# Decode attention with a gated block: the weight loads at the start cut into other pieces

## Chip, cores and metric

The kernel runs on one core of a Trainium2 chip. The core has five engines with an instruction stream each (TensorE "PE", VectorE "DVE", ScalarE "ACT", GpSimd "POOL", SyncE "SP") and sixteen DMA engines that move data between device memory (HBM) and on-chip memory. The metric is the device time of one execution in microseconds, the median of several runs.

## What is computed

One decode step for a batch of 8 tokens: a layer norm, attention of each token over the last 2048 positions of its key and value cache (32 query heads, 8 key heads), and a gated two-layer block whose result gates the attention's output. Everything large is bf16.

```
xn = layernorm(x)                                   # x: 8 x 1 x 512
q  = xn @ wq                                        # 512 x 4096, 32 heads of 128
k, v = k_cache[:, :, 6144:], v_cache[:, :, 6144:]   # 8 x 8 x 2048 x 128 each, used by 4 heads
s  = (softmax(q k^T / sqrt(128)) v) @ wo            # 4096 x 512
h  = sigmoid(xn @ w_gate) * (xn @ w_up)             # 512 x 1792
g  = silu(h @ w_down)                               # 1792 x 512
out = x + s * g
```

## The kernel before

**Loads.** All large loads are issued by SyncE (`q0`), in the order of a list `todo` written out by hand; only the small input x is issued by ScalarE (`q1`). A load of the list is issued when `pump` reaches it. Large tiles live in nine slots of 32 KB per partition (`slots`, `empty`); `free` gives a slot back when its last reader has been emitted, and `pump` then issues the next loads.

The list begins with the gated block's weights: `w_gate` (L171), `w_up` (L172), the first 11 x 128 rows of `w_down` (L173), and the remaining 384 rows of `w_down` in eight small loads (L174 to L183), between which lie the two halves of `wq` (L181). Then come the 16 tiles of the key cache and the 16 of the value cache, 2 MB each, the value tiles three places behind (L184 to L190), and at last `wo` in four pieces (L191).

`want_rows` (L96) takes a weight with `per` consecutive rows on each partition, and loads rows r0 to r1 of every partition, in steps of `step` rows. For `w_gate` and `w_up` there are four rows of 1792 per partition, and the step is 2: two loads of 2 x 1792 x 2 = 7168 bytes per partition each.

`want_side` (L122) loads one of the eight small parts of `w_down` into the tile `side`. A small part has 3, 5 or 9 partitions, each of 15 rows (15 KB) or 4 rows (4 KB); `sides` (L174) holds them as tuples. GpSimd clears the first 32 partitions of `side` before the first of them (L126), and that first small load waits for it.

**Semaphores.** Each load signals its completion on one of eight semaphores, taken in turn by all loads (x first). A load waits until the previous load on its semaphore has landed, besides the reader that frees its slot. So a load can only be issued when the one eight places ahead of it has landed.

**Compute.** The layer norm runs first (L212 to L242); then `g_ps` = gate (L278), `u_ps` = up (L294), the turning of h (L328), q (L352) and the down projection (L366). After that a loop over the batch (L647) transposes keys (L456), computes scores (L474), exponentials (L494) and the products with the values (L584). The output projection (L706) ends the kernel, when the last piece of `wo` is there.

Of the kernel before, what the change touches and what calls it, by code (L numbers as in the profile page):

```python
# [10 lines left out]
def kernel(  # L11
# [21 lines left out]
    KT = D // P  # L33
# [59 lines left out]
        empty.append(int(t[1][4:]))  # L93
        pump()

    def want_rows(name, w, per, r0, r1, step=None):  # L96
        def f(tag):
            t = slots.tile([P, r1 - r0, w.shape[1]], bf16, name=name, tag=tag)
            for a in range(r0, r1, step or r1 - r0):
                z = a + (step or r1 - r0)  # L100
                q0.dma_start(
                    out=t[:, a - r0 : z - r0, :],
                    in_=w.rearrange("(p r) n -> p r n", r=per)[:, a:z, :],
                )
            rows_of[(name, r0)] = (t, tag)
            for r in range(r0, r1):
                weights[(name, r)] = t[:, r - r0, :]

        todo.append((True, f))

    LOW, SF = (5, 5, 3, 3), 15
    MID, SM = 9, 4
    SP = 4 * max(LOW)
    M_AT = 32
    MP = 4 * MID
    MT = 11
    m0 = MT * P
    m1 = m0 + SF * sum(LOW)
    assert m1 + SM * MP == F
    side = {}  # L120

    def want_side(w, q, at, count, rows, base, of):  # L122
        def f(tag=None):
            if tag:
                t = slots.tile([P, SF, w.shape[1]], bf16, name="side", tag=tag)
                nc.gpsimd.memzero(t[:M_AT])  # L126
                side["t"] = t
                rows_of[("side", 0)] = (t, tag)
                for r in range(SF):
                    weights[("wd_sb", MT + r)] = t[: M_AT + MP if r < SM else SP, r]  # L130
            q0.dma_start(  # L131
                out=side["t"][at + q : at + q + 4 * (count - 1) + 1 : 4, :rows].rearrange(
                    "p s n -> p (s n)"
                ),
                in_=w[base : base + of * count * rows, :].rearrange(
                    "(p q s) n -> q p (s n)", q=of, s=rows
                )[q % of],
            )

        todo.append((not side, f))  # L140
        side["asked"] = True

    def want_down(w):
        def f(tag):
            t = slots.tile([P, MT, w.shape[1]], bf16, name="wd_sb", tag=tag)
            q0.dma_start(
                out=t[:].rearrange("p t n -> p (t n)"),
                in_=w[: MT * P, :].rearrange("(p t) n -> p (t n)", t=MT),
            )
            rows_of[("wd_sb", 0)] = (t, tag)  # L150
            for r in range(MT):
                weights[("wd_sb", r)] = t[:, r, :]

        todo.append((True, f))
# [13 lines left out]

    RT = 32
    Z = 32  # L170
    want_rows("wg_sb", B_w_gate, KT, 0, KT, 2)  # L171
    want_rows("wu_sb", B_w_up, KT, 0, KT, 2)  # L172
    want_down(B_w_down)  # L173
    sides = []  # L174
    for q in range(4):
        sides.append((q, 0, LOW[q], SF, m0 + q // 2 * 2 * LOW[0] * SF, 2))
        sides.append((q, M_AT, MID, SM, m1, 4))
    for x in sides[:2]:
        want_side(B_w_down, *x)
    for i in range(2):  # L180
        want_rows("wq_sb", A_wq, KT, 2 * i, 2 * i + 2)  # L181
        for x in sides[2 + 3 * i : 5 + 3 * i]:
            want_side(B_w_down, *x)  # L183
    order = [(b, i) for b in range(B) for i in range(NQ)]  # L184
    AHEAD = 3
# [5 lines left out]
    for t0, t1 in ((0, 16), (16, 26), (26, 30), (30, RT)):  # L191
# [15 lines left out]
        out=perm[:].rearrange("k (l p) -> k l p", l=G),  # L207
        in_=ident[:].rearrange("k (p l) -> k l p", l=G),
# [11 lines left out]
        out=rstd[:], in_=mv[:, 1:2], func=AF.Sqrt, bias=eps_t[:], scale=1.0  # L220
# [4 lines left out]
        out=xn_bf[:],  # L225
# [8 lines left out]
    for kt in range(KT):  # L234
        nc.tensor.transpose(  # L235
            out=xnT_ps[:, kt, :],
            in_=xn_bf[:].rearrange("b (p kt) -> b kt p", kt=KT)[:, kt, :],
# [25 lines left out]
    with nc.allow_low_precision(reason="zeros and a one"):  # L263
        nc.vector.reduce_sum(
            out=band[:], in_=ident[:].rearrange("k (q t) -> k q t", t=RT), axis=AX.X
        )
        nc.vector.reduce_sum(
            out=pick[:], in_=ident[:].rearrange("k (q t) -> k t q", t=RT), axis=AX.X
# [22 lines left out]
    for k in range(F // FC):  # L291
        u_ps = ps_t.tile([B, FC], f32, name="u_ps", tag="t")
        for kt in range(KT):
# [8 lines left out]
            out=h_bf[:B, k * FC : (k + 1) * FC],  # L302
# [6 lines left out]
    for h in range(2):  # L309
        c = LOW[2 * h]  # L310
        at = m0 + h * 2 * LOW[0] * SF
        nc.gpsimd.tensor_copy(
            out=h_side[:, :, : 4 * c].rearrange("b t (e q) -> b t e q", q=4)[
                :, :, :, 2 * h : 2 * h + 2
            ],
            in_=h_bf[:B, at : at + 2 * c * SF].rearrange(
                "b (e q t) -> b t e q", q=2, t=SF
            ),
        )
    nc.gpsimd.tensor_copy(  # L320
        out=h_side[:, :SM, M_AT:],
        in_=h_bf[:B, m1:F].rearrange("b (p t) -> b t p", t=SM),
    )
    cuts = [h_bf[:B, :m0].rearrange("b (p t) -> b t p", t=MT)[:, t] for t in range(MT)]
    rows = [P] * MT + [M_AT + MP] * SM + [SP] * (SF - SM)
    cuts += [h_side[:, t, : rows[MT + t]] for t in range(SF)]
    for t, x in enumerate(cuts):
        nc.tensor.transpose(  # L328
            out=hT_ps[: rows[t], t, :], in_=x, identity=ident[:B, :B]
# [45 lines left out]
    for e in range(2):  # L375
# [3 lines left out]
        for r in range(rep):  # L379
            nc.tensor.transpose(  # L380
                out=qT_ps[:, r].rearrange("p g z -> p (g z)"),
                in_=q_bf[:, r * Dh : (r + 1) * Dh],
# [3 lines left out]
            out=qm_sb[:, :, G * e : G * (e + 1), M0 : M0 + rep].rearrange(  # L386
                "p b g r -> p r g b"
            ),
            in_=qT_ps[:, :, :, :B],
# [14 lines left out]
    for j in range(NB):  # L404
# [15 lines left out]
        out=turn_rows[:].rearrange("k (x l r) -> k x l r", x=NU, l=G),  # L420
        in_=ident[:].rearrange("k (l x r) -> k x l r", x=NU, l=G),
    )
    sel_e = consts.tile([P, 2, Hq], f32, name="sel_e")
    for e in range(2):
        nc.vector.reduce_sum(
            out=sel_e[:, e, :].rearrange("k (i h) -> k i h", i=NQ),
            in_=ident_f[:].rearrange(
                "k (i m e h) -> k e i h m", i=NQ, m=NJ // 2, e=2
            )[:, e],
# [290 lines left out]
    for j in range(NB):  # L720
        (q0, q1)[j % 2].dma_start(
            out=out.flatten_outer_dims()[:, j * P : (j + 1) * P],
            in_=y_bf[Z * j : Z * j + B, :],
# [31 lines left out]
```

## Time and profile before

| what | value |
|---|---|
| time, median of 3 runs | 199.12 us (199.11 to 199.18) |
| the profiled execution's own time | 199.33 us |
| its span, first to last instruction | 197.5 us |
| PE busy | 157.4 us (80%) |
| DVE busy | 125.4 us (63%) |
| ACT busy, POOL busy | 40.7 us, 11.0 us |
| read from HBM | 81.01 MB, 410 GB/s over the span |
| mean granted TensorE clock | 0.965 |

The profile page divides the span into 40 slices of 4.94 us and gives for each the busy share of every engine and the rate of the DMA engines in GB/s. "The chain that ended last" follows the work back from the last instruction: each step names what released the next one. An entry such as "DMA v_sb" with 38 us in it is the time from the issue of that load to the moment when its reader could go on, and includes the time that it stood in the queue behind other loads. In a timeline, a row is a group of neighbouring instructions of one line: start, duration, engine, line, what, how many. "SPq" is SyncE issuing a load. The trace also records each DMA packet with its start, duration and size.

### The profile page before, as it was taken

Reading aid. Unit: us, or ns where it says so; the run is one execution under the profiler, and the core shown is the slowest. Engines: PE = TensorE matmul, PEld = TensorE weight load, DVE = VectorE, ACT = ScalarE, POOL = GpSimd, SP = SyncE. Lnnn points to the kernel's source line nnn. Section 1 sums busy time; section 2 is a strip of 40 time slices with the busy share of each in tenths; the row PEclk is TensorE's granted clock in tenths of the full one; section 3 lists DMA queues with packets and bytes.
Section 4 is the critical chain, followed back from the end, with each engine's and each line's share of the span. In section 5 each row is a group of like instructions: output and inputs, shape, how many; then the busy total and the mean of one; then the engine's idle time right before and its main releaser. Section 6 shows DMA issues by size and latency. Waiting matters only on the chain.

```text
span 197.5 us, 4796 instructions
## 1 busy us (share of the span) xinstructions
PE 157.4 (80%) x2112; PEld 103.1 (52%) x2112; DVE 125.4 (63%) x245; ACT 40.7 (21%) x95; POOL 11.0 (6%) x22
## 2 busy tenths in 40 slices
PE   0089559999788898799979987999799979976733
PEld 0034325776664565466545654566466556655531
DVE  4623106999797696679666965796669658935201
ACT  0522022006306001600160016001600160071000
POOL 8910200000000000000000000000000000000000
PEclk9999859999999999999999999999999999999975
DMA  6999999999999999999999999999999999999980
GB/s 205 424 440 435 431 434 435 425 425 431 423 425 425 438 428 435 431 425 428 422 433 431 435 425 433 428 418 428 428 438 431 428 428 431 428 423 425 428 366 21
DMA packets 6396, 81.32 MB, mean 412 GB/s; under 512 B 812, under 2 KB 820, under 8 KB 1624
## 3 DMA queue, kind: packets, MB, share of 16 engines
q1 hardware_dynamic: 6328, 81.01, 96.6%
q8 instruction: 16, 0.26, 0.5%
q10 hardware_dynamic: 48, 0.01, 0.0%
q14 instruction: 4, 0.03, 0.0%
HBM read 81.01 MB, written 0.01 MB: 410 GB/s over the span
## 4 chain that ended last, share of the span: by engine, by line
DMA 73%; PE 22%; POOL 3%; SPq 0%; issue 0%; DVE 0%; POOLq 0%
DMA v_sb<-in_A_v_cache_dram 46%; DMA wo_sb<-in_A_wo_dram 14%; PE kT_ps L456 11%; DMA wq_sb<-in_A_wq_dram 7%; DMA k_sb<-in_A_k_cache_dram 6%; PE o_ps L584 4%; PE s_ps L474 3%; POOL side L126 2%; PE m_ps L614 1%; PE fin_ps L706 1%; PE pT_ps L563 1%; SPq L131 0%; POOL perm L206 0%; POOL hT_sb L245 0%; DVE prod L717 0%
## 5 line engine op out<-in xcount | busy, mean ns | idle before, releaser
L461 DVE COPY kT_sb<-kT_ps 128x1024 bf16<-128x1024 bf16 x128 | 84.2, 683 | 28.9 <-PE kT_ps L456 25.0
L456 PE MATMUL kT_ps<-perm,k_sb 128*128 128x128 bf16 x1024 | 72.6, 220 | 3.7 <-DMA k_sb<-in_A_k_cache_dram 3.7
L456 PEld LDWEIGHTS <-k_sb 128*128 128x128 bf16 x1024 | 58.8, 98 | 26.1 <-issue 16.8
L584 PE MATMUL o_ps<-v_sb,pT_sb 128*32 128x256 bf16 (+1 forms) x352 | 36.5, 327 | 9.0 <-DMA v_sb<-in_A_v_cache_dram 7.6
L474 PE MATMUL s_ps<-kT_sb,qm_sb 128*32 128x512 bf16 x256 | 25.6, 389 | 1.3 <-DVE kT_sb L461 1.1
L494 ACT ACTIVATE p_buf<-s_ps,st 32x512 bf16<-32x512 f32 x32 | 21.7, 679 | 15.4 <-DVE st L487 15.1
L584 PEld LDWEIGHTS <-pT_sb 128*32 128x32 bf16 (+1 forms) x352 | 12.3, 101 | 21.7 <-issue 19.7
L604 ACT ACTIVATE o_sb<-o_ps,fac 128x512 f32<-128x512 f32 (+1 forms) x8 | 4.9, 608 | 60.9 <-PE o_ps L584 60.9
L568 DVE COPY pT_sb<-pT_ps 128x1024 bf16<-128x1024 bf16 x16 | 10.8, 676 | 1.8 <-PE pT_ps L563 1.8
L474 PEld LDWEIGHTS <-qm_sb 128*32 128x32 bf16 x256 | 7.0, 93 | 8.0 <-issue 1.3
L563 PE MATMUL pT_ps<-turn_rows,p_buf 128*128 128x128 bf16 x128 | 10.7, 227 | 0.0
L563 PEld LDWEIGHTS <-p_buf 128*128 128x128 bf16 x128 | 9.4, 149 | 0.2 <-issue 0.2
L521 ACT ACTIVATE w_row<-w 1x128 f32<-1x128 f32 x8 | 2.5, 309 | 30.6 <-DVE w L514 30.6
L235 PE MATMUL xnT_ps<-ident,xn_bf 8*128 8x8 bf16 x4 | 0.3, 176 | 10.6 <-DVE xn_bf L224 10.6
L385 DVE COPY qm_sb<-qT_ps 128x128 bf16<-128x128 bf16 x2 | 1.4, 881 | 8.7 <-PE qT_ps L380 8.7
L301 DVE TENSOR_TENSOR h_bf<-sig,u_ps 8x448 bf16<-8x448 f32 x4 | 2.4, 608 | 6.6 <-PE u_ps L294 6.1
L278 PE MATMUL g_ps<-wg_sb,xnT_sb 128*8 128x448 bf16 x16 | 5.7, 544 | 0.3 <-DVE xnT_sb L242 0.3
L494 ACT ACTIVATION_READ_ACCUMULATOR p_buf<-s_ps,st 32x1 f32 x32 | 5.9, 184 | 0.0
L706 PE MATMUL fin_ps<-wo_sb,oP_sb 128*32 128x128 bf16 x128 | 3.3, 263 | 3.1 <-DMA wo_sb<-in_A_wo_dram 3.1
L487 DVE TENSOR_REDUCE st<-s_ps 128x1 f32<-128x512 f32 x8 | 5.4, 681 | 0.5 <-PE s_ps L474 0.5
L235 PEld LDWEIGHTS <-xn_bf 8*128 8x128 bf16 x4 | 0.2, 117 | 10.6 <-DVE xn_bf L224 10.6
L352 PE MATMUL q_ps<-wq_sb,xnT_sb 128*32 128x512 bf16 x32 | 3.1, 526 | 3.2 <-DMA wq_sb<-in_A_wq_dram 3.2
(88 smaller groups left out, 92.0 us busy)
## 6 DMA issues: line engine op xcount, KB each, us to landing
k_sb<-in_A_k_cache_dram SPq DMA_DIRECT2D x16, 2048.0 KB
v_sb<-in_A_v_cache_dram SPq DMA_DIRECT2D x16, 2048.0 KB
wq_sb<-in_A_wq_dram SPq DMA_DIRECT2D x2, 2048.0 KB
wo_sb<-in_A_wo_dram SPq DMA_DIRECT2D x1, 2048.0 KB
wg_sb<-in_B_w_gate_dram SPq DMA_DIRECT2D x2, 896.0 KB
wu_sb<-in_B_w_up_dram SPq DMA_DIRECT2D x2, 896.0 KB
wd_sb<-in_B_w_down_dram SPq DMA_DIRECT2D x1, 1408.0 KB
wo_sb<-in_A_wo_dram SPq DMA_DIRECT2D x1, 1280.0 KB
```

The lines of the kernel that those rows point to most:

```text
L126: nc.gpsimd.memzero(t[:M_AT])
L278: nc.tensor.matmul(g_ps[:], lhsT=xnT_sb[:, kt, :B], rhs=weights[("wg_sb", kt)][:, k * FC : (k + 1) * FC], start=(kt == 0), stop=(kt == KT ...
L456: nc.tensor.transpose(out=kT_ps[:, c, :], in_=k_sb[:, j * CU + h * CH + c, :], identity=perm[:],)
L461: nc.vector.tensor_copy(out=kT[(b, u)][:, h * CH : (h + 1) * CH, :], in_=kT_ps[:])
L474: nc.tensor.matmul(s_ps[b][NR * l : NR * (l + 1), :], lhsT=qm_sb[:, b, i * G + l, o : o + Z], rhs=t[:, :, PG * l : PG * (l + 1)], start=(u ...
L487: nc.vector.tensor_reduce(out=st[b][:], in_=s_ps[b][:], axis=AX.X, op=ALU.max, negate=True)
L494: nc.scalar.activation(out=p_buf[b % 2][rows, :, l, :], in_=s[rows, :].rearrange("k (c p) -> k p c", p=PG), func=AF.Exp, bias=st[b][rows, ...
L563: nc.tensor.transpose(out=pT_ps[:, c, :], in_=p_buf[b % 2][:, :, :, h * CH + c].rearrange("k p l -> k (p l)"), identity=turn_rows[:],)
L568: nc.vector.tensor_copy(out=pT[b][:, h * CH : (h + 1) * CH, :], in_=pT_ps[:])
L584: nc.tensor.matmul(o_ps[r] if b < WIDE else o_ps[r, 0:2], lhsT=pT[b][:, c, r], rhs=x, start=(c == 0), stop=(c == CU - 1), tile_position=(0 ...
L604: nc.scalar.activation(out=o[:, :n], in_=o_ps[:, :n], func=AF.Copy, scale=fac.pop(b)[:])
L706: nc.tensor.matmul(fin_ps[Z * j : Z * (j + 1), :], lhsT=oP_sb[:, t, :], rhs=weights[("wo_sb", t)][:, j * P : (j + 1) * P], start=(t == 0), ...
```

## The change

`want_rows` takes a list of cuts instead of a step. `w_gate` is loaded in two pieces of one and three rows per partition (3584 and 10752 bytes), where it was two pieces of two rows; `w_up` is loaded in one piece of four rows (14336 bytes per partition), where it was two pieces. `want_side` takes a range of rows, and the last of the four small loads of 9 partitions x 4 rows is issued as two loads of 9 partitions x 2 rows. The rearranged address patterns name the same memory as one run per partition.

```diff
-    def want_rows(name, w, per, r0, r1, step=None):
+    def want_rows(name, w, per, r0, r1, cuts=()):
         def f(tag):
             t = slots.tile([P, r1 - r0, w.shape[1]], bf16, name=name, tag=tag)
-            for a in range(r0, r1, step or r1 - r0):
-                z = a + (step or r1 - r0)
+            for a, z in zip((r0, *cuts), (*cuts, r1)):
                 q0.dma_start(
-                    out=t[:, a - r0 : z - r0, :],
-                    in_=w.rearrange("(p r) n -> p r n", r=per)[:, a:z, :],
+                    out=t[:, a - r0 : z - r0, :].rearrange("p r n -> p (r n)"),
+                    in_=w.rearrange("(p r) n -> p r n", r=per)[:, a:z, :].rearrange(
+                        "p r n -> p (r n)"
+                    ),
                 )
...
-    def want_side(w, q, at, count, rows, base, of):
+    def want_side(w, q, at, count, rows, base, of, s0, s1):
...
             q0.dma_start(
-                out=side["t"][at + q : at + q + 4 * (count - 1) + 1 : 4, :rows].rearrange(
+                out=side["t"][at + q : at + q + 4 * (count - 1) + 1 : 4, s0:s1].rearrange(
                     "p s n -> p (s n)"
                 ),
-                in_=w[base : base + of * count * rows, :].rearrange(
-                    "(p q s) n -> q p (s n)", q=of, s=rows
-                )[q % of],
+                in_=w[base : base + of * count * rows, :]
+                .rearrange("(p q s) n -> q p s n", q=of, s=rows)[q % of][:, s0:s1]
+                .rearrange("p s n -> p (s n)"),
             )
...
-    want_rows("wg_sb", B_w_gate, KT, 0, KT, 2)
-    want_rows("wu_sb", B_w_up, KT, 0, KT, 2)
+    want_rows("wg_sb", B_w_gate, KT, 0, KT, (1,))
+    want_rows("wu_sb", B_w_up, KT, 0, KT)
...
-        sides.append((q, 0, LOW[q], SF, m0 + q // 2 * 2 * LOW[0] * SF, 2))
-        sides.append((q, M_AT, MID, SM, m1, 4))
+        sides.append((q, 0, LOW[q], SF, m0 + q // 2 * 2 * LOW[0] * SF, 2, 0, SF))
+        for s0, s1 in ((0, SM),) if q < 3 else ((0, SM // 2), (SM // 2, SM)):
+            sides.append((q, M_AT, MID, SM, m1, 4, s0, s1))
...
-        for x in sides[2 + 3 * i : 5 + 3 * i]:
+        for x in sides[2 + 3 * i : 5 + 4 * i]:
             want_side(B_w_down, *x)
```

## The prediction, made before the changed kernel was run

> **What bounds the kernel now.** I read the page first (slices, queues, the chain), then the chain of waits in order of time, then the first microseconds in stretches of half a microsecond, then SyncE's own issues, since the change touches only loads that SP issues.
>
> ```profile
> span 197.5 us, 4796 instructions
> ...
> GB/s 205 424 440 435 431 434 435 425 425 431 423 425 425 438 428 435 431 425 428 422 433 431 435 425 433 428 418 428 428 438 431 428 428 431 428 423 425 428 366 21
> ...
> q1 hardware_dynamic: 6328, 81.01, 96.6%
> ...
> DMA 73%; PE 22%; POOL 3%; SPq 0%; issue 0%; DVE 0%; POOLq 0%
> ```
>
> From the second slice to the thirty-eighth the rate hardly moves: 418 to 440 GB/s whether weights, keys or values are loaded. Queue q1 carries all of SP's loads, and its packets fill 96.6% of sixteen engines' span. Only the first slice (205) and the last two (366, 21) are not full. So the end is the start of the stream, plus 81 MB at the stream's rate, plus a short tail.
>
> ```profile
> 42.57 38.48 DMA v_sb<-in_A_v_cache_dram
> ...
> 163.50 28.32 DMA wo_sb<-in_A_wo_dram
> 191.82 0.04 issue
> 191.86 1.86 PE fin_ps L706 x52
> 193.72 0.02 issue
> 193.74 0.43 PE fin_ps L706 x8
> ```
>
> In the chain a load lands 38 or 28 us after its issue: it stood behind several others, so the queue was not empty when it came. The TensorE pieces between are only the way by which the chain got to an issue. At the end the last rows of wo arrive and PE has 2.3 us left.
>
> ```profile
> 1.50:2.00 0.50, 0.00 (x0) 0.00 (x0) 0.00 (x0) 0.00 (x0) 0.46 (x2) 1.00 1.24 158
> 2.00:2.50 0.50, 0.00 (x0) 0.00 (x0) 0.00 (x0) 0.00 (x0) 0.50 (x1) 1.00 0.30 74
> 2.50:3.00 0.50, 0.00 (x0) 0.00 (x0) 0.26 (x1) 0.00 (x0) 0.50 (x1) 1.00 0.95 272
> 3.00:3.50 0.50, 0.00 (x0) 0.00 (x0) 0.50 (x1) 0.00 (x0) 0.50 (x1) 1.00 0.81 315
> 3.50:4.00 0.50, 0.00 (x0) 0.00 (x0) 0.50 (x1) 0.00 (x0) 0.50 (x1) 1.00 1.00 416
> ```
>
> Last column GB/s. The stream ramps from 1.5 to 3.5 us, in which it moves (158 + 74 + 272 + 315) x 0.5 us = 410 KB, all from the first gate load. This is the one place where the form of the first load can count.
>
> ```profile
> 0.73 0.89 SPq L101 DMA_DIRECT2D wg_sb<-in_B_w_gate_dram  x2
> 1.66 1.35 SPq L101 DMA_DIRECT2D wu_sb<-in_B_w_up_dram  x2
> 3.06 0.63 SPq L146 DMA_DIRECT2D wd_sb<-in_B_w_down_dram  x1
> ...
> 12.04 0.34 SPq L101 DMA_DIRECT2D wq_sb<-in_A_wq_dram  x1
> 15.37 2.33 SPq L131 DMA_DIRECT2D side<-in_B_w_down_dram  x3
> 20.51 2.58 SPq L159 DMA_DIRECT2D k_sb<-in_A_k_cache_dram  x4
> 26.73 0.54 SPq L159 DMA_DIRECT2D v_sb<-in_A_v_cache_dram  x1
> ```
>
> This is SP's timeline; gaps between rows are SP waiting. An issue costs 0.34 to 0.86 us whatever the bytes.
>
> **The packets.** The trace's record of each packet gives the price of bytes and of pieces. One partition of a load is one packet. On a busy engine packets follow each other every 607 ns (16384 bytes), 381 (10240), 268 (7168), 155 (4096) and 80 (2048); a completion packet takes 9. A line through the longest and the shortest is (607 - 80) / (16384 - 2048) = 0.0368 ns a byte and 80 - 75.3 = 4.7 ns a packet. An engine carries 8 partitions of a 128-partition load; the 15 KB and 4 KB pieces of the small loads lie on some engines only. An engine with four of each has 32 x 0.268 + 8 x 0.418 + 280 x 0.607 + 8 x (0.381 + 0.155 + 0.080) + 4 x (0.569 + 0.155) + one instruction packet of 0.607 = 190.3 us of work, and the last packet of the run ends at 193.36. So these engines started, in effect, near 2.9 and were never idle; the first engine to end does so at 189.75. One engine whose first packet took 1.24 us (1.88 to 3.12) and which then ran at full pace has the effective start 3.12 - 0.27 = 2.85: such an engine sets the time.
>
> **Part 1: gate and up weights in pieces of 1, 3 and 4 rows instead of four of 2.** Per engine before: 32 packets x 268.2 = 8.58 us. After: 8 of 3584 bytes at 136.5, 8 of 10752 at 400, 8 of 14336 at 531.7 = 8.55. With one completion packet less that is -0.036 - 0.009 = -0.045 us on every engine, on the path.
>
> SP issues one up load instead of two: 0.63 to 0.68 us less, so wd is issued near 2.4 instead of 3.06. I cost this at nothing: the queue then holds 3.67 MB, 8.5 us of work, and the small load behind wd waits for GpSimd's memset (done at 5.07) in both versions. Without that cover the gain would be those 0.65 us. PE reads the gate weights at 11.12, released by xnT_sb, not by the load, and the up weights at 16.63; the up load ends its bytes near 11.3. So a later landing of the whole 14 KB delays nobody. Nor does an earlier one help.
>
> **Part 2: the ramp.** The trace has no first load with 3584-byte packets, so I bound it from both sides. The first packets took 0.56 to 1.41 us on most engines where a busy engine takes 0.27: they wait for first data. If that wait has a fixed length, an engine begins to stream at the same moment with either size: 0. Gain bound: the wait grows with the bytes asked for at once; the deciding engine waited 1.24 - 0.27 = 0.97, half of it is -0.49. Loss bound: in the ramp so many packets come through, not so many bytes; half of 410 KB is then missing, 205 KB at 432 GB/s = +0.47. I take 0: three engines have first packets of 0.27, two of the earliest 0.56 and 0.74, of the same size, so it is not the size that sets the wait. Both ends stay for the range.
>
> **Part 3: one small load in two halves.** Packets on the nine engines: 2 x 80 - 155 + 9 = +0.014 us, so there the sum of parts 1 and 3 is -0.03. On SP one issue more, 0.69 to 0.86 us (rows of 1.68, 3.27 and 2.33 for the eight before).
>
> **Part 4: the waits move.** Loads signal on eight semaphores in turn, and each new load waits for the one eight places before it. The count ahead of the first key load is unchanged (two gate, one up, nine small, against two, two, eight), so from the second pair of caches on every load waits for the same one. In between: the first wq load waits for none of them instead of x; the second wq load for the one up load instead of the second of two, both ending near 11.3 and issued near 12.0; the last half small load (new) for the first wq load, which lands at 20.5, and behind it on SP stands the first key load, which before waited for just that. So the first key issue moves from 20.51 to about 21.3. On the engines without small loads its first packet is due at 24.3, and issue to first packet is 1.04 us (0.73 to 1.77): 24.3 - 21.3 - 1.04 = 2.0 us of cover, by the rest of the second wq load. Hence 0; without cover, the whole 0.8. The fourth key load now waits for the second wq load (26.7) instead of a small one. Ahead of it are three key loads, 24 x 0.607 = 14.6 us from 24.3 on, so it isn't due before 38.9: 0. The first value load, next on SP, waited until 26.73 before and now goes about 0.6 later; nobody reads it before 60 us. PE, DVE, ACT and POOL keep their instructions and order.
>
> **Sum.** -0.03 to -0.045 us of 199.33, the profiled run's time (span 197.5 and 1.8 around it), which is 0.21 above the median of 199.12. Against the median that is 199.08; I say 199.05.
>
> **Rivals.**
> - Faster, 198.6: the ramp shortens, by up to the gain bound 0.49. For it: the three longest first packets (1.37, 1.41, 1.24) are nearly twice the others, which looks like engines in each other's way. Against: the early packet of 0.27. It decides if the engines with small pieces are those relieved.
> - Slower, 199.6: the ramp moves half as many bytes. Place: 1.77 to 3.5 us; price +0.47; it decides when second and third packets are as late as first ones. For it: second packets of 0.39 to 0.50 and thirds up to 0.74 on some engines. Against: most run at 0.27 from the second on.
> - Slower, 200.0 to 201.0: the first key load comes too late and every engine stops, 0.8 us, with 1.04 for a restart 1.8. It decides if that issue falls behind 23.2; I have it at 21.3.
> - Faster, 198.1: every load has a start of its own that shows, 1.04 us by the first one's issue to first packet, and there is one weight load less. Against: the ninth packet of an engine follows the eighth at the same 268 ns, across two loads, and 5 to 10 us shows 430 GB/s.
>
> For this last one there is a rule: the Trainium skill, "DMA: Bandwidth & Descriptors", section "Anatomy of one DMA", gives about 2.0 us fixed per transfer besides its bytes, and its section "Bandwidth" asks for 1 MiB or more per transfer. By it alone the merged up load would gain 2.0 us, an estimate from that page, and the time would be 197.1; the added small load would give the same back if it weren't hidden. The 430 GB/s across four loads of 0.9 MB speaks against the rule here: the fixed part lies beside other transfers.
>
> **How the numbers follow.** 0.2% is 0.4 us, about what a measurement of this kernel can tell from no change. Forecast 0.50 (own range 198.8 to 199.35); ramp shorter 0.23, ramp longer 0.20, late key load 0.05, starts showing 0.02. So faster 0.25, same 0.50, slower 0.25. The range takes in most of both ramp cases and leaves the rest: 198.5 to 199.7.
>
> **What would show it.** Right: the rate from 5 us on unchanged at about 430; first key issue near 21.3, and no dip from 24 to 30; the fourth key issue near 26.7; the last packet within 0.2 us of 193.36. The ramp rivals: the GB/s of the stretches 1.5 to 4 us, and the length of the first packets. A dip near 25 us would be the late key load. The forecast is wrong if the last wo row lands more than 0.4 us apart from before.

## The result, and the profile after

The changed kernel takes 199.44 us where the kernel before takes 199.19 (medians of 22 runs each): ratio 1.0013, 95% interval 1.0007 to 1.0019. That is +0.25 us, slower by less than the 0.2% that the prediction named as the bound of telling, but clear of its interval. The predicted time was 199.05: the measured one lies inside the predicted range (198.5 to 199.7), but on the other side of no change. The runs of the changed kernel also lie wider apart: 199.09 to 199.78, against 199.05 to 199.45 before.

The page of the changed kernel (profiled execution 199.64 us):

```profile
span 197.8 us, 4796 instructions
...
GB/s 203 428 433 435 437 426 424 431 427 424 419 434 431 431 431 431 431 424 424 434 426 427 441 431 423 424 427 434 421 447 427 424 427 427 434 423 431 420 357 16
...
q1 hardware_dynamic: 6202, 81.01, 96.5%
...
DMA 86%; PE 11%; SPq 1%; issue 0%; DVE 0%
```

The level of the rate from the second slice to the thirty-eighth is unchanged (419 to 447 GB/s), and the first slice has 203 instead of 205. To see how level it is, here is one stretch of 150 us, first before, then after (busy times of PE, PEld, DVE, ACT and POOL, then clock, DMA share, GB/s):

```profile
30.00:180.00 150.00, 133.73 (x1811) 89.81 (x1808) 112.37 (x219) 33.84 (x83) 0.00 (x0) 1.00 1.01 429
```

```profile
30.00:180.00 150.00, 134.88 (x1805) 90.45 (x1804) 112.40 (x219) 33.85 (x83) 0.00 (x0) 0.99 1.01 429
```

Both move 429 GB/s, though PE is busy 1.2 us more. One GB/s over this stretch would be 0.35 us, so the rows show no loss there but can't rule out one of 0.25 us; the finer measure below does. The end of the chain of waits in the changed kernel:

```profile
163.85 28.30 DMA wo_sb<-in_A_wo_dram
192.15 0.04 issue
192.19 1.85 PE fin_ps L708 x46
194.04 0.01 issue
194.05 0.43 PE fin_ps L708 x8
```

The tail from the first of these PE pieces on is as long as before (1.85 and 0.43 us of PE); all of it begins 0.33 us later (192.19 against 191.86). What came later is the end of the stream. Two places before 30 us differ. First the ramp, last column GB/s:

```profile
1.50:2.00 0.50, 0.00 (x0) 0.00 (x0) 0.00 (x0) 0.00 (x0) 0.45 (x2) 1.00 0.78 93
2.00:2.50 0.50, 0.00 (x0) 0.00 (x0) 0.00 (x0) 0.00 (x0) 0.50 (x1) 1.00 0.60 100
2.50:3.00 0.50, 0.00 (x0) 0.00 (x0) 0.08 (x1) 0.00 (x0) 0.50 (x1) 1.00 0.86 203
3.00:3.50 0.50, 0.00 (x0) 0.00 (x0) 0.50 (x1) 0.00 (x0) 0.50 (x1) 1.00 1.02 330
3.50:4.00 0.50, 0.00 (x0) 0.00 (x0) 0.50 (x1) 0.00 (x0) 0.50 (x1) 1.00 0.96 394
```

From 1.5 to 3.5 us it moves (93 + 100 + 203 + 330) x 0.5 us = 363 KB, where it moved 410 KB. 47 KB at 430 GB/s is 0.11 us. Second, SP's own timeline:

```profile
0.74 0.88 SPq L100 DMA_DIRECT2D wg_sb<-in_B_w_gate_dram  x2
1.66 0.59 SPq L100 DMA_DIRECT2D wu_sb<-in_B_w_up_dram  x1
2.29 0.68 SPq L147 DMA_DIRECT2D wd_sb<-in_B_w_down_dram  x1
...
12.05 0.34 SPq L100 DMA_DIRECT2D wq_sb<-in_A_wq_dram  x1
15.47 6.21 SPq L132 DMA_DIRECT2D side<-in_B_w_down_dram  x4
21.72 5.52 SPq L160 DMA_DIRECT2D k_sb<-in_A_k_cache_dram  x4
27.34 0.55 SPq L160 DMA_DIRECT2D v_sb<-in_A_v_cache_dram  x1
```

The last four small loads now take from 15.47 to 21.68, because the last half waits for the first wq load, and the first key load is issued at 21.72, where it was 20.51. In the 3 us in which the engines go over from wq to the keys, the rate falls from 418 GB/s (first row, before) to 402 (second row, after):

```profile
24.00:27.00 3.00, 0.29 (x4) 0.13 (x7) 0.00 (x0) 0.00 (x0) 0.00 (x0) 0.50 0.98 418
```

```profile
24.00:27.00 3.00, 0.33 (x4) 0.14 (x7) 0.00 (x0) 0.00 (x0) 0.00 (x0) 0.50 0.96 402
```

16 GB/s over 3 us are 48 KB, again 0.11 us. The prediction had costed both places at nothing.

**A finer measure.** The stretches above count a packet's bytes at its start, so a row of 0.5 us is rough. From the trace's packet records one can work out the delay of the mean engine at any moment: the time, less the work that was done by then (each packet at bytes / 27.2 + 4.7 ns, as in the prediction, summed and divided by sixteen). It gives for the profiled executions of all kernels that the verdict rests on (loads named in the section on the experiments):

| kernel | delay at 24 us | added 24 to 36 us | added 36 to 185 us | first key issue | last packet ends | its own time |
|---|---|---|---|---|---|---|
| before | 2.73 | 0.10 | 1.45 | 20.51 | 193.36 | 199.33 |
| before, second profile | 2.67 | 0.19 | 1.45 | 20.94 | 193.19 | 199.06 |
| changed | 2.82 | 0.19 | 1.45 | 21.72 | 193.71 | 199.64 |
| changed, second profile | 2.87 | 0.76 | 1.45 | 22.70 | 194.25 | 200.19 |
| gate 1 + 3 alone | 2.61 | 0.12 | 1.45 | 20.37 | 193.49 | 199.37 |
| gate 1 + 3, key early | 2.95 | 0.09 | 1.45 | 17.35 | 193.87 | 199.79 |
| halves alone | 2.56 | 0.46 | 1.45 | 21.46 | 193.49 | 199.50 |
| halves, key early | 2.67 | 0.09 | 1.45 | 17.15 | 193.26 | 199.31 |
| before, key early | 2.63 | 0.09 | 1.45 | 17.04 | 193.11 | 199.00 |
| up load alone | 2.50 | 0.36 | 1.45 | 20.50 | 193.21 | 199.16 |
| all but the gate pieces | 2.65 | 0.19 | 1.45 | 21.08 | 193.30 | 199.19 |
| the same, second profile | 2.70 | 0.58 | 1.45 | 21.60 | 193.90 | 199.73 |

The column "added 36 to 185 us" is the same in every row: what the mean engine loses, it loses before 36 us, and carries it to the end. The end itself is set by the engine that ends last, which in these executions ends 0.4 to 0.8 us after the mean of the sixteen. An execution's own time is its last packet's end plus 5.8 to 6.1 us. Single executions differ, so the verdicts below come from the medians, and this table only says where to look.

### The profile page after: what moved, and what is told of

It is laid out like the page before. It is cut to its first block, busy times and chain, and to the rows that moved or that the text cites. A ratio compares the mean times of both kernels' runs of the same rounds, so it can differ in the third digit from the quotient of the medians.

```text
span 197.8 us, 4796 instructions
## 1 busy us (share of the span) xinstructions
PE 158.9 (80%) x2112; PEld 103.9 (53%) x2112; DVE 125.2 (63%) x245; ACT 40.7 (21%) x95; POOL 11.0 (6%) x22
## 4 chain that ended last, share of the span: by engine, by line
DMA 86%; PE 11%; SPq 1%; issue 0%; DVE 0%
DMA v_sb<-in_A_v_cache_dram 30%; DMA k_sb<-in_A_k_cache_dram 30%; DMA wo_sb<-in_A_wo_dram 14%; DMA wq_sb<-in_A_wq_dram 7%; DMA wu_sb<-in_B_w_up_dram 5%; PE kT_ps L458 5%; PE o_ps L586 2%; PE fin_ps L708 1%; PE s_ps L476 1%; PE q_ps L354 1%; PE pT_ps L565 1%; PE m_ps L616 0%; SPq L100 0%; SPq L160 0%; DVE prod L719 0%
## 5 line engine op out<-in xcount | busy, mean ns | idle before, releaser
L463 DVE COPY kT_sb<-kT_ps 128x1024 bf16<-128x1024 bf16 x128 | 84.3, 684 | 29.1 <-PE kT_ps L458 24.3
L458 PEld LDWEIGHTS <-k_sb 128*128 128x128 bf16 x1024 | 59.5, 99 | 26.6 <-issue 18.0
L586 PE MATMUL o_ps<-v_sb,pT_sb 128*32 128x256 bf16 (+1 forms) x352 | 37.0, 330 | 7.8 <-DMA v_sb<-in_A_v_cache_dram 6.4
```

Of the source, the lines that this page charges most:

```text
L458: nc.tensor.transpose(out=kT_ps[:, c, :], in_=k_sb[:, j * CU + h * CH + c, :], identity=perm[:],)
L463: nc.vector.tensor_copy(out=kT[(b, u)][:, h * CH : (h + 1) * CH, :], in_=kT_ps[:])
L586: nc.tensor.matmul(o_ps[r] if b < WIDE else o_ps[r, 0:2], lhsT=pT[b][:, c, r], rhs=x, start=(c == 0), stop=(c == CU - 1), tile_position=(0 ...
```

## The experiments

Two theories were on trial. The *start theory*: the first gate load's small packets make the engines begin later or less evenly. The *late-key theory*: the extra small load and the moved waits make the first key load late, and the stream dips when wq runs out. In the first four expectations they are called ramp theory and late-load theory; the latter then took in the long packets of the up weights too. Each kernel was timed against the kernel before on the same chip, and the ratio to it is given with its 95% interval. Diffs are against the changed kernel.

### Which part of the change

Gate weights alone in pieces of 1 and 3 rows:

```diff
-    want_rows("wu_sb", B_w_up, KT, 0, KT)
+    want_rows("wu_sb", B_w_up, KT, 0, KT, (2,))
...
-        for s0, s1 in ((0, SM),) if q < 3 else ((0, SM // 2), (SM // 2, SM)):
+        for s0, s1 in ((0, SM),):
```

> The gate weights alone in pieces of 1 and 3 rows; up weights in two loads of 2 rows and the small load whole, as before. Number of loads and semaphores as before. Ramp theory (small first packets move fewer bytes while the first data is late, and the engines with the most small loads end later): +0.2 to +0.35 us against before, first key issue back at 20.5 us, last packet near 193.6 to 193.7. Late-load theory (the extra small load, the moved waits or the long up packets cost it): within 0.1 us of before.

Measured: 199.31 against 199.12, ratio 1.0011 (1.0002 to 1.0020), first key issue at 20.37. So +0.2 us without any late key load.

Everything but the gate pieces, in two runs:

```diff
-    want_rows("wg_sb", B_w_gate, KT, 0, KT, (1,))
+    want_rows("wg_sb", B_w_gate, KT, 0, KT, (2,))
```

> Everything of the change except the gate weights, which stay two loads of 2 rows. Ramp theory: within 0.1 us of before, although the first key issue is late as in the changed kernel (about 21.7 us). Late-load theory: +0.2 to +0.35 us.

> Everything of the change but the gate pieces, a second time, to narrow the first answer (+0.07 us, interval -0.1 to +0.25). Start theory: within 0.1 us of before, narrow spread. Late-key theory: +0.15 us or more.

Measured: 1.0003 (0.9994 to 1.0012) and 1.0006 (0.9997 to 1.0014). Neither is told from no change; both lean the same way, +0.07 and +0.08 us in the medians. After these the gate pieces looked like the whole story, which was too simple, as the next runs show.

The up weights in one load, and nothing else:

```diff
-    want_rows("wg_sb", B_w_gate, KT, 0, KT, (1,))
+    want_rows("wg_sb", B_w_gate, KT, 0, KT, (2,))
...
-        for s0, s1 in ((0, SM),) if q < 3 else ((0, SM // 2), (SM // 2, SM)):
+        for s0, s1 in ((0, SM),):
```

> The up weights in one load and nothing else of the change: gate weights in two loads of 2 rows, the small load whole, one load less than before, the first key load waits for the first wq load. Start theory: within 0.1 us of before. If the longer packets of the up weights cost anything: +0.1 us or more.

Measured: 1.0000 (0.9991 to 1.0009). This part does nothing, as predicted.

The last small load in two halves, and nothing else:

```diff
-    want_rows("wg_sb", B_w_gate, KT, 0, KT, (1,))
-    want_rows("wu_sb", B_w_up, KT, 0, KT)
+    want_rows("wg_sb", B_w_gate, KT, 0, KT, (2,))
+    want_rows("wu_sb", B_w_up, KT, 0, KT, (2,))
```

> The last small load in two halves and nothing else of the change: first key issue near 21.3 us. If the later first key load has a price in itself: +0.1 us or more, with single slow executions (as with 199.73 in the second run of the rest of the change); otherwise within 0.1 us of before.

Measured: 199.50 against 199.20, ratio 1.0019 (1.0007 to 1.0030), first key issue at 21.46. So the halves alone cost +0.3 us. Its stretch at the change from wq to keys has the lowest rate of the kernels shown so far:

```profile
24.00:27.00 3.00, 0.06 (x4) 0.05 (x7) 0.00 (x0) 0.00 (x0) 0.00 (x0) 0.50 1.01 386
```

386 GB/s against 418: 32 GB/s over 3 us are 96 KB, 0.22 us.

### The late key load, taken away and made larger

The halves again (gate and up weights as in the last diff), but with the first key load issued ahead of both:

```diff
+    last_sides = [todo.pop(-2), todo.pop()]
     AHEAD = 3
     for n in range(len(order) + AHEAD):
         if n < len(order):
             want_cache(k_tiles, A_k_cache, "k_sb", *order[n])
+            if n == 0:
+                todo.extend(last_sides)
```

> The last small load in two halves, nothing else of the change (that alone gave +0.30 us with the first key load at 21.46 us), but the first key load issued ahead of both halves, near 17.5 us. Late-key theory: within 0.1 us of before, no dip at 24 to 26 us. If the halves cost by their packets or their place in the queue: +0.2 us or more still.

Measured: 1.0006 (0.9997 to 1.0014). The key load's row in SP's timeline, then the stretch:

```profile
17.15 0.63 SPq L160 DMA_DIRECT2D k_sb<-in_A_k_cache_dram  x1
```

```profile
24.00:27.00 3.00, 0.31 (x4) 0.14 (x7) 0.00 (x0) 0.00 (x0) 0.00 (x0) 0.50 0.99 421
```

The issue is at 17.15 and the dip is gone (421 GB/s). The halves are the same two loads of the same packets; they only follow the first key load now. The packet records show what the dip is: in the halves alone, sixteen packets that start between 23.5 and 27 us take 0.7 to 1.28 us, where 0.61 is usual; with the key load early none takes over 0.61. Some sixteen packets are in flight all the while in both, so the engines do not run empty: single packets take longer. So what the halves cost, they most likely cost through the key load: 0.3 us falls to 0.05. The two intervals overlap (1.0007 to 1.0030 and 0.9997 to 1.0014), so it is the packets, more than the medians, that bear this out. The late issue is not the only way to such packets: the up load alone, with its key load issued at 20.50, has ten of them, up to 1.38 us.

Four pieces instead of two, as a larger dose (gate weights in two loads of 2 rows, up weights in one):

```diff
-        for s0, s1 in ((0, SM),) if q < 3 else ((0, SM // 2), (SM // 2, SM)):
+        for s0, s1 in ((0, SM),) if q < 3 else tuple((s, s + 1) for s in range(SM)):
...
-        for x in sides[2 + 3 * i : 5 + 4 * i]:
+        for x in sides[2 + 3 * i : 5 + 6 * i]:
```

> A larger dose of late key load: gate weights in two loads of 2 rows, up weights in one, the last small load in four loads of one row, all but the first ahead of the first key load and behind the first wq load. Late-key theory: first key issue near 23 us, deep dip from 24 to 26 us, +0.4 us or more against before. Start theory: within 0.1 us of before.

Measured: 1.0086 (1.0073 to 1.0099), +1.7 us, with the first key issue at 22.73. A second wait had moved in this kernel that the expectation did not name: the second key load now waits for the second wq load, so the price is not that of one late load alone.

The changed kernel with the key load ahead of the last half, and then instead with the last small load whole:

```diff
+    last_side = todo.pop()
...
             want_cache(k_tiles, A_k_cache, "k_sb", *order[n])
+            if n == 0:
+                todo.append(last_side)
```

```diff
-        for s0, s1 in ((0, SM),) if q < 3 else ((0, SM // 2), (SM // 2, SM)):
+        for s0, s1 in ((0, SM),):
```

> The changed kernel with the first key load issued ahead of the last half small load, so that it waits only for the first wq load as before. Late-key theory (the stream dips at 24 to 26 us because the first key load comes 1.2 us later, worth about 0.1 us of the mean engine in the changed kernel): first key issue back near 20.5 us, dip mostly gone, 0.1 us or more faster than the changed kernel (+0.05 to +0.2 us against before remain). Start theory alone (the first gate load makes the start of the engines later or more uneven, nothing else costs): +0.2 to +0.3 us as the changed kernel.

> The changed kernel with the last small load whole: one load less, the first key load waits for the first wq load as before. Late-key theory: as the run with the key load ahead, 0.1 us or more faster than the changed kernel. Start theory: about +0.2 us against before, as the run with the gate weights alone in 1 and 3 rows (+0.2).

Measured: 1.0017 (1.0008 to 1.0025) with the key issue at 20.44, and 1.0010 (1.0002 to 1.0019) with it at 20.97. Neither is faster than the changed kernel's 1.0013 by anything that can be told. So with the gate pieces in place, the late key load does not explain the loss.

The key load early in the kernel before (the first of the last two diffs, on gate and up weights in two loads of 2 rows each and the small load whole):

> The kernel before with one thing else: the first key load is issued ahead of the last small load, so it waits for the second small load and not for the first wq load: first key issue near 17.7 us instead of 20.5. If lateness of the first key load costs the kernel before anything, this is faster than before by up to 0.1 us (the mean engine loses 0.02 us from 24 to 32 us before); if not, within 0.1 us of it.

Measured: 0.9999 (0.9990 to 1.0008). The kernel before has the cover it needs; there is nothing to gain.

### The start, alone and made larger

The gate pieces with the key load early (the same order of loads, up weights in two loads and the small load whole, with the gate weights in 1 and 3 rows):

> The same order of loads with the gate weights in pieces of 1 and 3 rows (up weights in two loads, the small load whole): the first key load has 3 us more cover. Start theory: still +0.15 us or more against before, and a wide spread of the runs (about 199.0 to 199.8). Late-key theory (an uneven start only matters because the fastest engines run dry before the first key load is there): within 0.1 us of before, and a narrow spread.

Measured: 199.50 against 199.17, ratio 1.0015 (1.0006 to 1.0023), runs from 199.26 to 199.79. SP's row, the stretch at the change to keys, and the ramp:

```profile
17.35 0.63 SPq L160 DMA_DIRECT2D k_sb<-in_A_k_cache_dram  x1
```

```profile
24.00:27.00 3.00, 0.00 (x0) 0.00 (x0) 0.00 (x0) 0.00 (x0) 0.00 (x0) 0.50 0.98 416
```

```profile
1.50:2.00 0.50, 0.00 (x0) 0.00 (x0) 0.00 (x0) 0.00 (x0) 0.46 (x2) 1.00 0.40 67
2.00:2.50 0.50, 0.00 (x0) 0.00 (x0) 0.15 (x1) 0.00 (x0) 0.50 (x1) 1.00 1.05 165
2.50:3.00 0.50, 0.00 (x0) 0.00 (x0) 0.50 (x1) 0.00 (x0) 0.50 (x1) 1.00 0.81 186
3.00:3.50 0.50, 0.00 (x0) 0.00 (x0) 0.50 (x1) 0.00 (x0) 0.50 (x1) 1.00 1.08 301
```

The key load is 3 us earlier than before and the stretch at 24 us is within 2 GB/s of before, yet the time is 0.3 us longer. So the gate pieces cost time with the other place out of play. In this execution, the longest of its run, the loss is in the ramp, which moves (67 + 165 + 186 + 301) x 0.5 = 360 KB, 50 KB less than before.

The gate pieces alone do not show it that way. Here is the ramp of that execution in one row:

```profile
1.50:3.50 2.00, 0.00 (x0) 0.00 (x0) 1.14 (x1) 0.00 (x0) 1.96 (x2) 1.00 0.83 230
```

230 GB/s over 2 us are 460 KB, more than the 410 of before, and the delay at 24 us is 2.61, less than before. The sixteen engines' last packets end at 192.75 us on average, against 192.77 before; only the last one ends late, 0.74 us after that average (0.60 and 0.41 in the two profiles of before). So a late start of the mean engine is not in every execution of the gate pieces, and one profile can't say what makes the time of this one.

The changed kernel a second time, without an edit:

> The changed kernel itself, on the chip of this call: +0.25 us against before, wide spread. A second profile of one execution: the start theory expects that its time goes with the end of its slowest engine, and not that the first 3.5 us look the same in both.

Measured: 1.0014 (1.0005 to 1.0023). The profiled execution was one of its longest, 200.19 us, and shows what the two places make together:

```profile
22.70 6.01 SPq L160 DMA_DIRECT2D k_sb<-in_A_k_cache_dram  x4
```

```profile
24.00:27.00 3.00, 0.00 (x0) 0.00 (x0) 0.00 (x0) 0.00 (x0) 0.00 (x0) 0.50 0.92 347
```

The start was late (2.87 in the table), so the first wq load landed late, so the last half and the key load behind it went out at 22.70, and the rate fell to 347 GB/s: 71 GB/s over 3 us are 213 KB, 0.5 us.

Two small gate loads, then one of two rows, with the small load whole and the up weights in one load:

```diff
-    want_rows("wg_sb", B_w_gate, KT, 0, KT, (1,))
+    want_rows("wg_sb", B_w_gate, KT, 0, KT, (1, 2))
```

> A larger dose of small first packets: gate weights in pieces of 1, 1 and 2 rows, up weights in one load, the small load whole (as many loads as before, first key load waits as before). Start theory: +0.2 us or more against before. Late-key theory: within 0.1 us of before.

Measured: 1.0015 (1.0001 to 1.0028), runs from 198.95 to 200.41. The profiled execution was the longest; in its packet records some 15.2 packets are in flight from 4.75 to 6 us, where 16.2 are before and after (neighbours overlap a little): one engine moves nothing.

Other first pieces, the last small load in halves:

```diff
-    want_rows("wg_sb", B_w_gate, KT, 0, KT, (1,))
+    want_rows("wg_sb", B_w_gate, KT, 0, KT, (3,))
```

```diff
-    want_rows("wg_sb", B_w_gate, KT, 0, KT, (1,))
-    want_rows("wu_sb", B_w_up, KT, 0, KT)
+    want_rows("wg_sb", B_w_gate, KT, 0, KT, ())
+    want_rows("wu_sb", B_w_up, KT, 0, KT, (2,))
```

> The changed kernel with the gate weights in pieces of 3 and 1 rows: the first load's packets have 10752 bytes, the bytes and the number of loads are the same. Ramp theory in its plain form (a packet's wait is fixed, so longer first packets carry more through the ramp): faster than the changed kernel by 0.25 us or more, and 0 to 0.2 us faster than before. Late-load theory: as the changed kernel, +0.25 us. If small first packets have nothing to do with it but the order or moment of the second load does, anything else.

> Gate weights in one load of 14336-byte packets, up weights in two of 2 rows, the small load in two halves: as many loads as in the changed kernel and the same waits, longest first packets. Ramp theory in its plain form: 0.1 to 0.4 us faster than before. Late-load theory: +0.25 us.

Measured: 1.0008 (0.9999 to 1.0017), which is not told from no change, and 1.0033 (1.0021 to 1.0044). The plain form of the start theory, that longer first packets carry more through the ramp, fell: 14336-byte first packets are the worst of the four sizes that were tried. In that kernel three engines' first packets took 1.5 to 2.2 us, where before none took more than 1.41, and the dip at the key load is there as well, so its +0.7 us is not the price of the first load alone.

### Packet size or size of the first load: not settled

The first two rows of the gate weights in two loads of 64 partitions each (`p0` to `p1` is a range of partitions; the cut is at row 2, the up weights are one load, the small load is whole):

```diff
-                q0.dma_start(
-                    out=t[:, a - r0 : z - r0, :].rearrange("p r n -> p (r n)"),
...
+                parts = ((0, P // 2), (P // 2, P)) if name == "wg_sb" and a == 0 else ((0, P),)
+                for p0, p1 in parts:
+                    q0.dma_start(
+                        out=t[p0:p1, a - r0 : z - r0, :].rearrange("p r n -> p (r n)"),
+                        in_=w.rearrange("(p r) n -> p r n", r=per)[
+                            p0:p1, a:z, :
```

> First load as small in bytes as in the changed kernel (448 KB) but with packets of 7168 bytes: rows 0 and 1 of 64 partitions, then of the other 64, then rows 2 and 3 of all; up weights in one load, the small load whole, as many loads as before. If the size of the packets is what makes the start late: within 0.1 us of before (up to +0.1 for the rest of the change), narrow spread. If it is that the first load is small and the second one's packets come later: +0.2 us or more, wide spread as with 1 and 3 rows.

Measured: 1.0088 (1.0068 to 1.0108). While these loads run, the rate is about half, in the trace from 2 us on (last column):

```profile
2.00:4.00 2.00, 0.00 (x0) 0.00 (x0) 1.70 (x1) 0.00 (x0) 2.00 (x1) 1.00 0.99 254
4.00:6.00 2.00, 0.00 (x0) 0.00 (x0) 1.97 (x2) 0.00 (x0) 2.00 (x4) 1.00 1.04 229
6.00:8.00 2.00, 0.00 (x0) 0.00 (x0) 0.26 (x3) 1.62 (x3) 2.00 (x3) 1.00 0.98 340
```

so this says nothing about the question. The same with even and odd partitions, `slice(0, P, 2)` and `slice(1, P, 2)`:

> First load of 448 KB in packets of 7168 bytes again, now rows 0 and 1 of the even partitions, then of the odd ones, then rows 2 and 3 of all, so that the 64 partitions of a load lie over the whole memory (with the lower 64 the rate was only 205 to 285 GB/s). If the size of the packets makes the start late: within 0.1 us of before, narrow spread. If the small first load does: +0.2 us or more, wide spread. A rate near 240 GB/s from 2 to 7 us would make it inconclusive again.

Measured: 1.0075 (1.0055 to 1.0094). Here the rate was full from 3.5 us on:

```profile
3.50:4.50 1.00, 0.00 (x0) 0.00 (x0) 1.00 (x1) 0.00 (x0) 1.00 (x1) 1.00 1.04 430
```

But one packet too few was in flight from 4.75 to 6 us, as in the run with two small gate loads, and one engine's last packet ended at 195.40, 1.5 us after the next engine's. Both runs have three gate loads, where the changed kernel has two, and most of the loss here is that one engine: the next one ends at 193.88, against 193.36 for the last one before. So this run does not tell the size of the packets from the size of the first load either; which property of the first loads matters stays open.

The second profile of the kernel before:

> The kernel before, for a second profile of one execution. Start theory: the mean engine's start, worked out from the packets up to 8 us, is between 2.60 and 2.75 us as in the other profiles with first packets of 7168 bytes (2.63 to 2.73), below most of those with 3584 bytes (2.60 to 2.95, and 3.06 with two such loads).

Measured: 2.66 at 8 us, in the expected band. Over nine profiles with gate loads of 2 + 2 rows the delay at 24 us is 2.50 to 2.73 us, mean 2.64; over six with 1 + 3 rows, 2.61 to 2.95, mean 2.79. So the mean engine starts 0.15 us later on average with the small first load, and from one execution to the next less alike; two of the six (2.61 and 2.68) lie among the nine.

## Why the prediction was wrong

**Right.** What bounds the kernel: the delay added from 36 to 185 us was 1.45 us in every kernel of the table. The price of packets: on a busy engine of the changed kernel 14336-byte packets follow each other every 532 ns and 10752-byte packets every 400, as forecast; the gain of 0.045 us from them is too small to be seen. The up weights in one load: nothing (1.0000), so the rival in which every load has a start of its own that shows, 1.04 us, is out. The Trainium skill's fixed cost of about 2.0 us a transfer ("DMA: Bandwidth & Descriptors", section "Anatomy of one DMA") is given there for transfers that GpSimd issues; these are issued by SyncE, so that estimate did not apply, and the merge of two loads in one busy queue gained none of it. The order of the waits was right too: second wq load at 12.05, the last half behind the first wq load, the fourth key load at 26.71, the first value load at 27.34. One sum is off without touching the forecast, which is a difference: 193.36 less 190.3 is 3.06, not 2.9, and the engines were not at their best pace throughout, as the 1.45 us show.

**Wrong, part 2: "I take 0".** This is the step that failed: the change of the first load was costed at nothing, and it costs 0.2 to 0.3 us. The argument was that packets of one size show very different first waits, so size does not set the wait. That they differ is true, but it does not say that the distribution stays when the load changes. Measured: +0.2 to +0.3 us in the time with the gate pieces alone (1.0011, and 1.0015 with the key load early), and +0.15 us for the start of the mean engine, on average over fifteen profiles. All six measurements of kernels with gate pieces of 1 + 3 rows, the result among them, lie clear of no change (1.0010 to 1.0017), whether the key load is late or not; of the six with 2 + 2 rows on all partitions, the run with four pieces left aside, only the halves alone do. The loss bound of +0.47 held. The rival that the prediction called "the ramp moves half as many bytes" came true in kind in the changed kernel, at less than its price: 363 of 410 KB, not half. Why a smaller first load makes the start later, and why one execution of the gate pieces alone lost time without it, stays open.

**Wrong, part 4: "2.0 us of cover".** The place was right, but the cover was mis-sized. It took 1.04 us, the first load's time from issue to first packet, as the lead that a load needs. Measured: with the first key load issued at 21.46 us, 2.8 us before its first packet is due (24.3), the rate is down by 32 GB/s over 3 us and the time is +0.3 us; with 7 us of lead there is no dip. So 1.04 us was too little. How much is enough is not settled. With 3.8 us, as before, there is next to no loss (0.10 us added from 24 to 36 us, where 0.09 is the least of all), and with 3.4 us, in the second profile of before, 0.1 us more. But the changed kernel, issued at 21.72, added only 0.19, and the up load alone, issued at 20.50 as before, added 0.36. The issue was also 0.4 us later than forecast (21.72, not 21.3). In the time of the changed kernel this place is not seen: with the key load moved forward it stays at 1.0017 and 1.0010.

**The signs that it named.** The rate from 5 us on was as it said. The dip from 24 to 30 us came, though it was to stay away, and the last packet ended 0.35 us late (193.71 against 193.36), outside the 0.2 that would have been right and inside the 0.4 that it called wrong. That the time fell inside the range is due to the loss bound of the ramp, which the range took in, not to the forecast.

**The sum.** The two losses do not add: +0.2 to +0.3 from the gate pieces and +0.3 from the halves, each alone, make +0.25 together, and the halves with the merged up load only +0.07 and +0.08. The intervals of single runs are about 0.2 us wide on either side, so part of this may be chance, the +0.3 of the halves alone above all. One reading is that a stream that starts later also needs the key load later, so the first loss hides part of the second. The up load alone fits it: its execution started early (2.50), added 0.27 us more than the least at the key load with the issue unchanged at 20.50, and ended as before. The second profile of the changed kernel does not: it started late (2.87) and lost most at the key load (0.76), since there the key load was late too. So this stays open.

## What to carry to other kernels

In a kernel that is one long stream of loads, look at its seams: the first microseconds, and each place where a load is issued because another one landed. For the lead that a load needs, do not take an idle queue's time from issue to first packet (1.04 us here, where 2.8 was too little in one kernel); look at how early the loads are issued at seams where the rate holds. And where a start varies from run to run, one profile of each kernel shows little: compare several, and put the verdict on medians.

## What the runs showed of the hardware

A load on partitions 0 to 63 or 64 to 127 alone ran at 229 to 254 GB/s, about half of the 430 that loads on all partitions reach, though all sixteen engines were busy (DMA share 0.99 to 1.04). Loads on every second partition ran at full rate (430 GB/s from 3.5 to 4.5 us), so it is the half that matters, not the number of partitions.

A load that comes late to a busy stream need not leave an engine idle: in the halves alone sixteen packets take 0.7 to 1.28 us instead of 0.61, with sixteen in flight throughout. In the second profile of the changed kernel, with the key load issued at 22.70, engines did run empty: 9 to 10 packets were in flight from 24.5 to 25 us.

The start of the stream depends on the shape of the first load in a way that no simple rule of packet size gives: gate weights in 2 + 2 rows were the best of the shapes tried, 1 + 3 cost +0.2 to +0.3 us, 3 + 1 with the rest of the change cost +0.15 us, which is not told from nothing, and with three gate loads an engine stood still for over 1 us in two of three profiles. Why an engine waits there, no view of the profile shows.
